# Scaled expert inputs made by GpSimd instead of VectorE, and begun earlier from the fourth token pair on

## The chip, the cores and the metric

One core of a Trainium2 chip. The metric is device time in microseconds (us) of one execution of the whole program, lower is better. Engines are named as in the profile: PE (TensorE: matmuls, with PEld for its weight loads), DVE (VectorE), ACT (ScalarE), POOL (GpSimd), SP (SyncE, here only a DMA queue). Each engine works through its own instruction stream in order; semaphores tie the streams together.

## What is computed

Two stages, the second on the output of the first:

```python
# 1. attention: q, k, v of shape (4, 8, 768, 64); causal. Heads 0, 2, 6 see all keys
#    before the query, the others 4 sink keys and a window of 64 keys.
a = softmax(where(mask, q @ k.T / 8, -1e9));  attn = a @ v
# 2. four experts over x = attn as (3072, 512); w1 (4, 512, 1024), w2 (4, 1024, 512)
p = domain_probs / (domain_probs.sum(-1, keepdims=True) + 1e-9)
for e in range(4):
    h = np.maximum(x @ w1[e], 0.0)
    out += p[:, e:e + 1] * (h @ w2[e])
```

Since p is not negative, p * relu(x @ w1) = relu((p * x) @ w1). The kernel uses this: for most tokens it multiplies the input by the expert's p ahead of the first layer, and then adds up all experts in one product of the second layer.

## The kernel before

**Tokens.** 3072 tokens are 24 tiles of 128. The attention runs in eight groups of three tiles (four batches, two halves each). Tiles 0 to 3 go through the experts in a plain way; the other twenty go in ten pairs of two tiles, in the code by their first tile: `pairs = [4, 6, ..., 22]`. The program works on the experts of one pair while it works on the attention of a later group: their matmuls are interleaved on PE in an order that Python code writes out by hand (`manual_schedule`: each engine gets its instructions in the order in which the code emits them). Each `yield` of the generators `moe_steps` and `attention` lets the other go on, by a plan with a due time for each attention group.

**A pair** (`pair_steps`). Layer 1 runs expert by expert: `plain_layer1` for experts 0, 1, 2 and, for expert 3 (and in the last three pairs for more of them), `winograd_layer1`, a Strassen-Winograd form with seven products instead of eight. Layer 2 is one such form over all experts: six `product` calls of 16 matmuls of 256 columns and a seventh one, with sums on DVE in between.

**Scaled inputs** (`scale_inputs`). For a pair and an expert, xs = xT * pB: xT is the attention's output, transposed, in fp16 (one tile per attention group), pB the pair's probabilities for all partitions in fp32. One instruction of 128 x 1024 elements, or two of 512 where the pair lies in two groups (pairs 8, 14, 20). `xs` has three slots: experts 0 and 2 share one, expert 1 has the second, expert 3 the third. So expert 2's input may be written only when PE has read expert 0's. In the last pairs expert 2 goes to a tile of its own, `xs1`, that takes the room of q's tile, and in the last two expert 1 goes into a part of `vS`. `scaled_sums` makes sums of an expert's scaled input on DVE for the Winograd form. `pB` has one buffer: `load_probs` of the next pair on SP waits until this pair's last input is made.

In the kernel before, the inputs of experts 0 and 3 of the next pair are made on DVE after the fifth and the sixth product of layer 2, those of experts 1 and 2 within layer 1 of the pair (in the last pairs somewhat differently).

**POOL** issues the attention's loads as DMAs: when the code takes up a group it calls `loads`, three DMAs for `k_rows` (L219), three for `q` (L219), three for `vR` (L304); after each window head's product of probabilities and values it calls `load_v` for the next group's `vS` (L306, five for a group). A vS load waits until PE has read that head's old values (L828). SP transposes k, q and the attention's output by DMA (`transpose_rows`, L790) and stores the results.

Lines that come up later: L1180 the scaling, L1196, L1204 and L1014 sums and differences on DVE, L1229 and L1258 the matmuls of layer 1 (plain, Winograd), L1409 those of layer 2, L693 the attention's scores, L756 and L828 its values, L718 and L722 its masks.

Of the kernel before, what the change touches and what calls it, by code (L numbers as in the profile page):

```python
# [19 lines left out]
def kernel(  # L20
# [33 lines left out]
    nc = tc.nc  # L54
# [43 lines left out]
    gp = nc.gpsimd  # L98
# [15 lines left out]
    EW = (E - 1, E - 2)  # L114
# [291 lines left out]
    for h in range(H):  # L406
# [16 lines left out]
        eng = nc.scalar if h < HP else nc.sync  # L423
# [131 lines left out]
    def mm_ns(cols):  # L555
        return cols / 2.4 + 2.5
# [444 lines left out]
    S2, S3, S4 = A11, A21, A12  # L1001
# [141 lines left out]
    def pieces(nt0):  # L1143

        g0, j0 = divmod(nt0, 3)
        n0 = min(3 - j0, PT)
        yield g0, j0 * P, 0, n0
        if n0 < PT:
            yield g0 + 1, 0, n0, PT - n0
# [16 lines left out]
        x = xs_of[0][:, n * DMP * PC : (n + 1) * DMP * PC]  # L1166
        return x.rearrange("p (c x) -> p c x", c=DMP)

    def scale_inputs(nt0, e):

        if xs_of[0] is None:
            xs_of[0] = moe.tile([P, XS], FP16, name="xs", tag="xs", bufs=1)
        xs = scaled(e)
        for g, c0, t0, n in pieces(nt0):
            require(g)
            xin = xT[g][:, :, c0 : c0 + n * P].rearrange("p c (t x) -> p c t x", t=n)
            o = xs[:, :, t0 * P : (t0 + n) * P].rearrange("p c (t x) -> p c t x", t=n)
            pb = pB_of[nt0][:, t0 : t0 + n, e, :]
            pb = pb.rearrange("p t (c x) -> p c t x", c=1)
            nc.vector.tensor_tensor(  # L1180
                out=o, in0=xin, in1=pb.to_broadcast([P, DMP, n, P]), op=ALU.mult
            )

# [30 lines left out]

    def two(nt0):
        return nt0 >= pairs[-LAST]

    def three(nt0):
        return nt0 >= pairs[-2]

    def pair_steps(nt0, nxt):
# [93 lines left out]
        a, b = (winograd_layer1(e, *y) for e, y in zip(EW, (banks, banks[::-1])))  # L1315
        if three(nt0):
# [5 lines left out]
            b = winograd_layer1(EW[1], *more_banks, more_kept)  # L1322
# [19 lines left out]
        if not two(nt0):  # L1342
            n = itertools.chain(*(plain_layer1(e) for e in range(E - 1)))
            order = (
                ((n,), lambda: scale_inputs(nt0, 1)),
                ((n,), more[0] if more else None),
                ((n, a), lambda: last_weight_sum(E - 1) if nt0 == pair0 else None),
                ((n, a), None),
                ((n, a), lambda: scale_inputs(nt0, 2)),
                ((n, a), lambda: load_probs(nxt)),  # L1350
                ((n, a), more[1] if more else None),
                ((n, a), more[2] if more else None),
                ((n, a), lambda: first_sum(0, 2)),
                ((n,), None),
                ((n, n), lambda: first_sum(2, 2)),
                ((), lambda: scale_inputs(nxt, 1) if two(nxt) else None),
            )
        elif nxt is None:
            order = (
                ((), lambda: scaled_sums(EW[1])),  # L1360
                ((a, b, a, b), None),
                ((a, b, a, b), lambda: scaled_sums(EW3)),
                ((a, b, a, b, a, b), lambda: scaled_sums(0)),
                ((third, fourth, third, fourth), lambda: first_sum(EW[0])),
                ((third, fourth, third, fourth), lambda: first_sum(EW[1])),
                ((third, fourth, third, fourth), None),
                ((third, fourth), lambda: (first_sum(EW3), first_sum(0))),
            )
        elif three(nt0):
            n = plain_layer1(0)  # L1370
            order = (
                ((), lambda: scaled_sums(EW[1])),
                ((a, b, a, b), lambda: load_probs(nxt)),
                ((a, b, a, b), None),
                ((a, b, a, b), None),
                ((a, b), lambda: scaled_sums(EW3)),
                ((n,), more[0]),
                ((third, third, n), lambda: first_sum(EW[0])),
                ((third, third, n), more[1]),
                ((third, third, n), lambda: (first_sum(EW[1]), first_sum(0))),  # L1380
                ((third,), lambda: (first_sum(EW3), more[2]())),
            )
        else:
            n = itertools.chain(plain_layer1(0), plain_layer1(1))
            order = (
                ((a, a, n), more[0] if more else None),
                ((a, a, n), lambda: load_probs(nxt) if nxt else None),
                ((a, a, n), more[1] if more else None),
                ((n,), lambda: scaled_sums(EW[1])),
                ((a, b, n), more[2] if more else None),  # L1390
                ((b, b, n), lambda: first_sum(0)),
                ((b, b, n), lambda: first_sum(EW[0])),
                ((b, n, b), lambda: (first_sum(1), first_sum(EW[1]))),
            )
# [9 lines left out]
        x = pO.tile([P, DM], FP32, name="pO", bufs=2)[:, 0:HN]  # L1404
        y = pO.tile([P, DM], FP32, name="pO", bufs=2)[:, 0:HN]

        def product(ps, a, b, first, middle=None):
            for k in range(KT):
                nc.tensor.matmul(  # L1409
                    out=ps,  # L1410
                    lhsT=a[:, k, :],
                    rhs=b(k),
                    start=(first and k == 0),
                    stop=(k == KT - 1),
                    skip_group_check=not first,
                )
                if k == KT // 2 - 1:
                    if middle is not None:
                        middle()
                    yield KT // 2 * mm_ns(HN), PSHARE  # L1420

        def b(k, n):
            return lambda kt: whole_b(k, n, kt // HT, kt % HT)
# [17 lines left out]
        def second_sum(n):  # L1441
            k = slice(n * KT // 2, (n + 1) * KT // 2)
            minus(S2[:, k, :], S1[:, k, :], A11[:, k, :])

        def third_sum(n):

            k = slice(n * KT // 2, (n + 1) * KT // 2)
            minus(S3[:, k, :], A22[:, k, :], S2[:, k, :])

        def fourth_sum(n):  # L1450
            k = slice(n * KT // 2, (n + 1) * KT // 2)
            minus(S4[:, k, :], A12[:, k, :], S2[:, k, :])

        last = nxt is None
        ahead = nxt and two(nxt)
        if ahead and three(nxt):
            inputs_for_third()
        half = KT // 2 * mm_ns(HN), PSHARE
        yield from product(x, A11, b(0, 0), True)
        keep(0, x)  # L1460
        second_sum(0)
        yield half
        yield from product(y, A12, b(1, 0), True, lambda: second_sum(1))
        add(0, y, 0, 0)
        if ahead and two(nt0):
            scale_inputs(nxt, 1)
        yield half
        yield from product(x, S2, t(1), False, lambda: third_sum(0))
        keep(1, x)
        third_sum(1)  # L1470
        yield half
        yield from product(y, S1, t(0), True, lambda: fourth_sum(0))
        keep(2, y)
        fourth_sum(1)
        yield half
        yield from product(
            x, S3, b(0, 1), False, lambda: scale_inputs(nxt, EW[0]) if ahead else None
        )
        add(2, x, 1, 1)
        if last:  # L1480
            keep(3, x)
        else:
            scale_inputs(nxt, 0)
        yield half
        yield from product(
            y, S4, b(1, 1), False, lambda: scaled_sums(EW[0]) if ahead else None
        )
        add(1, y, 0, 1)
        if nxt is not None:
            scale_inputs(nxt, EW[1] if ahead else EW[0])  # L1490
        store(0)
        if last:
            store(1, 1)
# [28 lines left out]
    pairs = list(range(pair0, NTILE, PT))  # L1522

    def moe_steps():

        sums = []
        for e in range(E):
            n0 = (e % 2) * FTP * CH
            for n, step in enumerate(plain_steps(0, 3, e, lambda: xT[0], n0)):
                yield step  # L1530
                if e == 0 and n == FTP // 2:
                    prob_rows()
                if sums and n >= FTP and n % 2 == 0:
                    sums.pop(0)()
            sums = weight_sums(e)
        for x in sums:
            x()
        sums = first_weight_sums(EW[0])
        for e in range(E):
            n0 = (e % 2) * FTP * P  # L1540
            for n, step in enumerate(plain_steps(3, 1, e, lambda: xT[1][:, :, 0:P], n0)):
                yield step
                if n == FTP - 1:
                    sums[e]()
            if e + 1 < E:
                last_weight_sum(e)
                (
                    lambda: scale_inputs(pairs[0], 0),
                    lambda: scale_inputs(pairs[0], EW[0]),
                    lambda: scaled_sums(EW[0]),  # L1550
                )[e]()
        for n, nt0 in enumerate(pairs):
            yield from pair_steps(nt0, pairs[n + 1] if n + 1 < len(pairs) else None)
# [114 lines left out]
```

## Time and profile before

| what | value |
|---|---|
| time, median of 3 runs | 376.0 us (375.86 to 377.12) |
| span of the profiled execution | 376.1 us |
| granted TensorE clock, mean | 1.000 |
| PE busy | 367.1 us, 98% |
| DVE busy | 281.6 us, 75% |
| ACT busy | 227.3 us, 60% |
| POOL busy (with the issue of its DMAs) | 112.9 us, 30% |
| L1180 on DVE | 49 instructions into xs, 47.0 us; 3 into vS, 2.5 us |
| POOL's loads of vS (L306) | 30, of 0.99 us each; 110.5 us of waits for PE in front of them |

The profile is of one execution and its span agrees with the runs. Its page has the busy time of each engine, the chain of work that ended last and the costliest groups of instructions; further answers of the trace are the timeline of a stretch (start, duration, engine, line, operation, output<-inputs, and in brackets the idle time before it and what ended it), the busy time by stretches of the run, and the waits of one engine (who waited for whom: us in total, times, longest).

### The profile page before, as it was taken

How to read it: one execution, taken by the hardware profiler on the slowest of the kernel's cores; microseconds unless marked ns; L12 is line 12 of the kernel's file. 1: busy time of each engine (PE TensorE's matmuls, PEld its weight loads, DVE VectorE, ACT ScalarE, POOL GpSimd, SP SyncE). 2: the span in 40 equal slices, each digit the busy share in tenths (PEclk: the TensorE clock that was granted, in tenths of full speed). 3: DMA queues.
4: the chain of work that ended last, by engine and by line, in shares of the span. 5: the costliest groups of instructions: out<-in, count | busy, mean ns of one | idle time of the engine just before them, and what ended most of it. 6: DMA issues, size and time to landing. Idle time of an engine off the chain costs nothing.

```text
span 376.1 us, 10310 instructions
## 1 busy us (share of the span) xinstructions
PE 367.1 (98%) x4221; PEld 312.4 (83%) x4221; DVE 281.6 (75%) x589; ACT 227.3 (60%) x475; POOL 112.9 (30%) x155
## 2 busy tenths in 40 slices
PE   8889999999999999999999999999999999999996
PEld 4755556568998999999989899988899998998996
DVE  7774768697788569868657858957767968989882
ACT  3863478557785785765676955774678362450630
POOL 8923664793058038115601650320000000000000
DMA  8999999999599579988904991971220200300101
GB/s 157 159 208 207 179 186 194 180 201 121 90 104 164 97 83 133 153 111 63 205 12 61 169 156 16 131 129 12 68 72 2 92 24 2 114 2 0 58 3 58
DMA packets 123748, 39.25 MB, mean 104 GB/s; under 512 B 113728, under 2 KB 116356, under 8 KB 123700
## 3 DMA queue, kind: packets, MB, share of 16 engines
q0 software_dynamic: 85824, 19.01, 58.6%
q1 hardware_dynamic: 36276, 19.18, 23.3%
q8 instruction: 33, 0.54, 0.7%
q10 hardware_dynamic: 1600, 0.39, 0.5%
q14 instruction: 15, 0.12, 0.1%
HBM read 44.89 MB, written 6.34 MB: 136 GB/s over the span
## 4 chain that ended last, share of the span: by engine, by line
PE 78%; DMA 12%; DVE 5%; POOL 3%; issue 1%; ACT 0%; DVEq 0%; POOLq 0%
PE pO L1409 29%; PE pA L1229 20%; PE pO L1258 9%; PE pO L1116 5%; DMA q<-in_q_dram 5%; PE pA L693 4%; DMA w2sb<-in_moe_w_dram 4%; PE pA L1095 3%; DMA w1sb<-in_moe_w_dram 2%; PE pV L1258 2%; PE pA L1258 2%; DVE xs L1180 2%; PE pV L828 2%; PE pV L756 2%; DMA xT<-x_pair 1%
## 5 line engine op out<-in xcount | busy, mean ns | idle before, releaser
L1409 PEld LDWEIGHTS <-hA 128*128 128x128 f16 x1104 | 104.9, 98 | 11.9
L1229 PE MATMUL pA<-xs,w1sb 128*128 128x256 f16 x768 | 97.1, 272 | 0.0
L1229 PEld LDWEIGHTS <-w1sb 128*128 128x128 f16 x768 | 71.7, 98 | 7.3
L1409 PE MATMUL pO<-w2sb,hA 128*128 128x256 f16 x640 | 76.8, 272 | 0.0
L711 ACT ACTIVATE es<-pA 128x384 f16<-128x384 f32 (+2 forms) x122 | 59.2, 512 | 26.4 <-PE pA L693 23.2
L1238 ACT ACTIVATE hA<-pA 128x512 f16<-128x512 f32 x96 | 57.2, 597 | 29.6 <-PE pA L1229 27.3
L306 POOL DMA_DIRECT2D vS<-in_v_dram x30 | 29.6, 986 | 113.7 <-PE pV L828 110.5
L1409 PE MATMUL pO<-tsb,hA 128*128 128x256 f16 x464 | 56.8, 272 | 0.0
L1180 DVE TENSOR_TENSOR xs<-xT,pB 128x1024 f16<-128x1024 f16 (+1 forms) x49 | 47.0, 977 | 3.7 <-DMA xT<-x_pair 3.7
L1014 DVE TENSOR_TENSOR hA<-hA 128x1024 f16<-128x1024 f16 x60 | 39.4, 684 | 0.6 <-PE pO L1409 0.3
L1108 ACT ACTIVATE hA<-pA 128x384 f16<-128x384 f32 (+1 forms) x64 | 22.2, 385 | 20.3 <-PE pA L1095 20.2
L1258 PEld LDWEIGHTS <-w1sb 128*128 128x128 f16 x512 | 31.3, 98 | 2.1 <-DVE xs L1014 0.8
L1095 PE MATMUL pA<-xT,w1sb 128*128 128x384 f16 (+1 forms) x256 | 30.4, 272 | 2.0 <-DMA w1sb<-in_moe_w_dram 1.9
L1116 PE MATMUL pO<-w2sb,hA 128*128 128x512 f16 x128 | 30.6, 379 | 0.1
L1095 PEld LDWEIGHTS <-w1sb 128*128 128x128 f16 x256 | 19.5, 98 | 11.0 <-issue 2.6
L1429 ACT COPY s<-pO 128x256 f32<-128x256 f32 x31 | 11.5, 372 | 27.3 <-PE pO L1409 21.8
L851 DVE TENSOR_TENSOR xT<-pV,rc 64x384 f16<-64x384 f32 x37 | 20.5, 554 | 9.3 <-ACT rc L856 6.8
L722 DVE TENSOR_TENSOR es<-es,mS 128x384 f16<-128x384 f16 (+1 forms) x40 | 13.8, 344 | 18.0 <-ACT es L711 17.9
L846 ACT ACTIVATE rc<-pV,eps 64x384 f32<-64x384 f32 x37 | 21.3, 575 | 7.0 <-PE pV L828 6.4
L1275 DVE CUSTOM_DVE_ANT_0 hA<-pO,s 128x512 f16<-128x512 f32 x26 | 17.7, 688 | 9.9 <-PE pO L1258 8.5
L1268 ACT COPY s<-pO 128x512 f32<-128x512 f32 x39 | 22.7, 588 | 3.2 <-PE pO L1258 3.0
L693 PE MATMUL pA<-qT,kR 128*128 128x128 f16 (+2 forms) x141 | 23.1, 261 | 0.4 <-DVE kR L602 0.4
(170 smaller groups left out, 527.6 us busy)
## 6 DMA issues: line engine op xcount, KB each, us to landing
pB<-p_rows SPq DMA_DIRECT2D x10, 512.0 KB
out_dram<-o SPq DMA_DIRECT2D x19, 256.0 KB
w1sb<-in_moe_w_dram POOLq DMA_DIRECT2D x8, 512.0 KB, 9.2
w2sb<-in_moe_w_dram POOLq DMA_DIRECT2D x4, 1024.0 KB, 13.3
vS<-in_v_dram POOLq DMA_DIRECT2D x30, 112.0 KB, 4.8
k_rows<-in_k_dram POOLq DMA_DIRECT2D x18, 128.0 KB, 5.1
q<-in_q_dram POOLq DMA_DIRECT2D x18, 128.0 KB, 6.4
vR<-in_v_dram POOLq DMA_DIRECT2D x24, 48.0 KB, 5.5
```

The lines of the kernel that those rows point to most:

```text
L306: gp.dma_start(out=t[:, :, own_v(h)], in_=windows_of(v, b, h, c))
L693: nc.tensor.matmul(out=ps[:, o : o + nq], lhsT=key_tile(b, c, h, t), rhs=qTs[b, c][:, hp, q0 : q0 + nq], start=(n == 0 or not first), stop ...
L711: nc.scalar.activation(out=es[:, 0:cols], in_=ps[:, 0:cols], func=AF.Exp, scale=SC)
L1014: nc.vector.tensor_tensor(out=out, in0=a, in1=b, op=ALU.subtract)
L1095: nc.tensor.matmul(out=pss[ft][:, 0:cols_n], lhsT=w1_tile(e, ct, ft), rhs=x[:, ct, :], start=(n == 0), stop=(n == DMP - 1),)
L1116: nc.tensor.matmul(out=ps_o, lhsT=hs[:, ft, j * P : (j + 1) * P], rhs=w2sb[:, e * FTP + ft, :], start=(ft == 0), stop=(ft == FTP - 1),)
L1180: nc.vector.tensor_tensor(out=o, in0=xin, in1=pb.to_broadcast([P, DMP, n, P]), op=ALU.mult)
L1229: nc.tensor.matmul(out=ps[:, f * PC : (f + 1) * PC], lhsT=w1_tile(e, ct, f0 + f), rhs=xs[:, ct, :], start=(ct == 0), stop=(ct == DMP - 1),)
L1238: nc.scalar.activation(out=blocks[:, b0 : b0 + 2, k0 : k0 + 2, :].rearrange("p t f x -> p f t x"), in_=ps.rearrange("p (f t x) -> p f t x" ...
L1258: nc.tensor.matmul(out=ps[:, f * P : (f + 1) * P], lhsT=w_tile(e, w[:, ct, :], f), rhs=a[:, ct, :], start=(first and f == 0 and ct == 0), ...
L1268: nc.scalar.copy(out=kept[n], in_=ps)
L1409: nc.tensor.matmul(out=ps, lhsT=a[:, k, :], rhs=b(k), start=(first and k == 0), stop=(k == KT - 1), skip_group_check=not first,)
```

## The change

The scaling goes from DVE to POOL, save for the two inputs of the first pair (experts 0 and 3) that are made during the plain tiles. And the places where the code emits it are another: the list `to_scale` holds what is to be made for the next pair during layer 2 of this one. For the pairs 6 and 8 these are experts 3 and 0, in the middle of and after the fifth product. For pairs from 10 on (`ahead_of`), they are emitted after the first, third and fourth product, and expert 1's is among them; for the last pairs also expert 2's, in the middle of the fifth product or after it.

```diff
-    def scale_inputs(nt0, e):
+    def scale_inputs(nt0, e, eng=None):
...
-            nc.vector.tensor_tensor(
+            (eng or gp).tensor_tensor(
                 out=o, in0=xin, in1=pb.to_broadcast([P, DMP, n, P]), op=ALU.mult
             )
...
+    def ahead_of(nt0):
+
+        return nt0 >= pairs[3]
...
-                ((n,), lambda: scale_inputs(nt0, 1)),
+                ((n,), lambda: None if ahead_of(nt0) else scale_inputs(nt0, 1)),
...
+        to_scale = []
+        if nxt is not None:
+            to_scale = [EW[0], 0]
+            if ahead:
+                to_scale += [EW[1], 1] if two(nt0) else [EW[1]]
+            elif ahead_of(nxt):
+                to_scale += [1]
+
+        def scale_one(after):
+            if to_scale and (after or ahead_of(nxt)):
+                scale_inputs(nxt, to_scale.pop(0))
+
         yield from product(x, A11, b(0, 0), True)
         keep(0, x)
         second_sum(0)
+        scale_one(False)
         yield half
         yield from product(y, A12, b(1, 0), True, lambda: second_sum(1))
         add(0, y, 0, 0)
-        if ahead and two(nt0):
-            scale_inputs(nxt, 1)
         yield half
         yield from product(x, S2, t(1), False, lambda: third_sum(0))
         keep(1, x)
         third_sum(1)
+        scale_one(False)
         yield half
         yield from product(y, S1, t(0), True, lambda: fourth_sum(0))
         keep(2, y)
         fourth_sum(1)
+        scale_one(False)
         yield half
-        yield from product(
-            x, S3, b(0, 1), False, lambda: scale_inputs(nxt, EW[0]) if ahead else None
-        )
+        yield from product(x, S3, b(0, 1), False, lambda: scale_one(True))
         add(2, x, 1, 1)
         if last:
             keep(3, x)
         else:
-            scale_inputs(nxt, 0)
+            scale_one(True)
...
         add(1, y, 0, 1)
-        if nxt is not None:
-            scale_inputs(nxt, EW[1] if ahead else EW[0])
...
-                    lambda: scale_inputs(pairs[0], 0),
-                    lambda: scale_inputs(pairs[0], EW[0]),
+                    lambda: scale_inputs(pairs[0], 0, nc.vector),
+                    lambda: scale_inputs(pairs[0], EW[0], nc.vector),
```

In the built program the streams of PE, ACT and SP hold the same instructions in the same order as before. 50 instructions of L1180 have left DVE's stream; the rest of it is unchanged. On POOL's stream they stand between the DMAs, in this order for the pairs by their first tile (numbers are experts; "loads" are the nine DMAs of k_rows, q and vR of the next group, "vS" one load of L306):

```
pair 4:   loads, 1, 2
pair 6:   vS x5, 3, loads, 0, 1, 2
pair 8:   vS x5, loads, 3, 0, 1, 2      (each in two halves)
pair 10:  3, vS, 0, vS, 1, vS x3, loads, 2
pair 12:  3, 0, 1, vS x4, 2, vS, loads
pair 14:  3, 0, 1, vS x2, 2, vS x2      (each in two halves)
pair 16:  3, vS, 0, 1, 2
later:    no loads between them
```

## The prediction

> **What bounds the kernel now.** I read first the page's busy times and the share of each stretch, then the waits of PE, then the chain, then the queue orders around the moved instructions, and last the timeline at each place where a moved result is read.
>
> ```profile
> PE 367.1 (98%) x4221; PEld 312.4 (83%) x4221; DVE 281.6 (75%) x589; ACT 227.3 (60%) x475; POOL 112.9 (30%) x155
> ...
> 80.00:110.00 30.00, 30.00 (x373) 25.75 (x372) 24.08 (x51) 20.78 (x50) 10.31 (x13) 1.00 1.09 129
> ...
> 230.00:260.00 30.00, 29.52 (x362) 26.74 (x360) 23.57 (x56) 19.23 (x38) 4.94 (x5) 1.00 0.66 89
> ...
> PE pO L1258 <- DVE xs L1014: 0.5, 1, 0.5
> PE pO L1258 <- ACT hA L1308: 0.2, 1, 0.2
> ```
>
> PE is the bound, and really so: in the pairs it is busy for whole stretches (second number of a stretch), and the chain steps at one rate (48 matmuls of 256 columns in 5.24 us at 253.47, 112 in 12.23 us at 310.55: 109 ns each). From 80 us on PE waits 0.5 us for DVE once and 0.2 us for ACT once; those two lines are the whole list. So relieving DVE can win 0.7 us at most, 0.2% of 376. Less than 0.3% (1.1 us) can't be told from no change here. What can move the time is a new wait of PE.
>
> **What the change moves.** 50 of the 52 instructions of L1180 (47.0 us for 49 by the page's group, 2.5 us for the three into vS) leave DVE for POOL; the first pair's inputs of experts 0 and 3 stay. The order of PE, ACT and SP is as before. DVE loses 26 whole pieces of 1.21 us and 24 half pieces of 0.68 us, 48 us that stand beside PE: worth 0, bound 0.7. The cost is where they go: POOL also issues the attention loads, in order, and holds each until PE has freed its buffer.
>
> **The price of one on POOL.** No row shows a product of two inputs there. From below: DVE's own 1.21 us. From above: GpSimd's select, one input, took 654 ns for 504 elements (1.30 ns each); if two inputs are read one after the other, 1024 elements take 2.66 us. I take the middle between one stream (1.33) and two (2.66), 2.0 us, as GpSimd need not slow a select and a product alike; half pieces by DVE's ratio 0.68/1.21, 1.12 us. The Trainium skill (GPSIMD Engine Reference, § 3.1 Elementwise) has a 2048-element product-like add at 4497 ns, 1.96 times VectorE; an estimate from it is 2.2 us, and the time below would be 0.9 us more.
>
> ```profile
> L1180 DVE TENSOR_TENSOR xs<-xT,pB 128x1024 f16<-128x1024 f16 (+1 forms) x49 | 47.0, 977 | 3.7 <-DMA xT<-x_pair 3.7
> ...
> L491 POOL TENSOR_SCALAR_AFFINE_SELECT mS<-mS 128x504 f16<-128x504 f16 x1 | 1.0, 985 | 0.1
> L487 POOL TENSOR_SCALAR_AFFINE_SELECT mS<-mS 128x504 f16<-128x504 f16 x1 | 0.7, 654 | 0.1
> ```
>
> **Second pair (tiles 6, 7).** On POOL's new queue stand: five vS loads, expert 3's input, nine loads (k_rows, q, vR: three each), then the inputs of experts 0, 1, 2. PE's first matmul of the pair reads expert 0's.
>
> ```profile
> 112.08 0.98 POOL L306 DMA_DIRECT2D vS<-in_v_dram  x1 [0.46 <-issue]
> ...
> 113.06 2.65 POOL L219 DMA_DIRECT2D k_rows<-in_k_dram  x3
> ...
> 115.33 1.23 DVE L1180 TENSOR_TENSOR xs<-xT,pB 128x1024 f16<-128x1024 f16 x1 [0.55 <-DMA xT<-x_pair]
> ...
> 115.67 2.66 POOL L219 DMA_DIRECT2D q<-in_q_dram  x3
> ...
> 118.27 2.39 POOL L304 DMA_DIRECT2D vR<-in_v_dram  x3
> ...
> 118.81 1.91 PE L1229 MATMUL pA<-xs,w1sb 128*128 128x256 f16 x16
> ```
>
> The bracket at 115.33 is the point: DVE stood idle there until the last transpose of xT landed, so no engine can scale this pair earlier. Now POOL waits to 115.33 with expert 3's input (done at 117.3, before DVE's sums want it at 118.21), and the nine loads behind it, which began at 113.06 and took 7.60 us in a row (to 120.66), follow. Expert 0's input is done at 115.33 + 2.0 + 7.60 + 2.0 = 126.9; PE wants it at 118.81. New wait: 8.1 us. Expert 1 then follows 2.0 later, 3.2 before PE reaches it (5.2 after its first, 124.05); expert 2 likewise fits. The loads land some 4 us later and PE is 8.1 later, so nobody waits for them.
>
> **Third pair (8, 9).** Here all nine loads stand ahead of all its inputs, each in halves (its tiles are of two attention groups).
>
> ```profile
> 144.35 2.65 POOL L219 DMA_DIRECT2D k_rows<-in_k_dram  x3
> ...
> 146.84 1.28 DVE L1180 TENSOR_TENSOR xs<-xT,pB 128x512 f16<-128x512 f16 x2
> 146.96 2.66 POOL L219 DMA_DIRECT2D q<-in_q_dram  x3
> ...
> 149.55 1.91 PE L1229 MATMUL pA<-xs,w1sb 128*128 128x256 f16 x16
> 149.55 2.33 POOL L304 DMA_DIRECT2D vR<-in_v_dram  x3
> ```
>
> The loads follow a vS load that PE frees, so they keep their place relative to PE. They end at 151.88; two halves of expert 3 and two of expert 0 take 4 x 1.12: 156.4, wanted at 149.55. New wait: 6.8 us. DVE's sums of expert 3 and the masks queued behind them wait less than PE does.
>
> **From the fourth pair on.** The products in front give cover; I checked each reader. Fourth: experts 3, 0, 1 stand among vS loads and are done near 173 for a reader at 178.16; expert 2 behind the loads (end 184.53) at 186.5 for 188.27. That cover is 1.7 us: gone if a piece costs over 3.7. Fifth: 198 for 209.70; its expert 2 must wait for PE to leave the slot (213.98) and holds one vS and nine loads by 3 us, landing near 231 for transposes at 233. Sixth: 231 for 238.51; its expert 2 goes into q's old room, free only where DVE began at 247.18 before, done by 249.4 for a reader at 249.19: 0 to 0.2, against the 0.5 us wait for DVE that goes: 0. It holds two vS loads to 249, whose buffer is read only after the sink rows of 269. Seventh to tenth: five or more us early. First pair: 89.8 for 93.44 and 94.8 for 99.38. SP's pB load of the next pair waits for POOL's last input of this one (expert 2), in the fourth pair 1.8 us longer than for DVE's; what stands behind it on SP is an xT transpose of 197.31, twelve us on, and the pB itself is wanted by the early products only, so nothing is late.
>
> **After a stall.** PE has no row of a pause over 1.3 us in its work. Its nearest long rest is the one ahead of its first matmul, and there it ran at half rate:
>
> ```profile
> 1.27 3.59 PE L448 MATMUL pO<-early 128*128 128x512 f16 x8 [1.27 <-DVE early L433]
> ...
> 69.90 4.32 PE pO L1116 x20
> ```
>
> Eight matmuls of 512 columns from 1.27 to 4.73, 0.43 us each, against 0.216 later; full rate from about 6.5. That costs half of 5.2 us, 2.6. After the 1.1 us wait at 21.5 the rate was full. Bounds for each stall: 0 to 2.6; stalls of 8 and 7 us resemble the rest more than the 1.1 us wait, so I take 2.6 twice, 5.2. The Trainium skill (TensorE: Matmul & The Clock Gate, Part 1) says the same of the sign: an idle window of about 3.4 us halves the clock until about 3.4 us of sustained work; by that figure it would be 1.7 twice, 1.8 us less in all. The trace's start agrees (half rate, for 5.2 us); no run here shows it within the work.
>
> **Sum.** Profiled execution 376.1 us, median of the runs 376.0, so nothing lies around the span; from the median: 376.0 + 8.1 + 6.8 + 5.2 = 396.1, said as 396.
>
> **Rivals.**
> *Stalls without the half rate*: 376.0 + 14.9 = 390.9. For it: the 1.1 us wait cost nothing afterwards. Against: the start.
> *DVE and POOL hold each other up.* DVE's two sums at 75.64 took 2.17 us beside L491 of POOL, where L1014 has 0.684 each: 0.8 lost. If in each of the seven later pairs one sum on PE's path loses that, 5.6 more: 401.7. Against: DVE is given 48 us. The Trainium skill (SBUF — State Buffer, Who interferes with whom) states it as a rule: a VectorE instruction with two SBUF inputs and a GpSimd instruction that reads SBUF exclude one another; the row agrees.
> *Not slower: loads do not hold the scaling.* If POOL only hands a load over and computes beside its 0.8 to 1 us, the nine loads cost nothing: second pair 115.33 + 4.0 = 119.3 for 118.81, third 145.7 (xT written) + 4.5 = 150.2 for 149.55; 1.2 us, less up to 0.7: 376.5. It decides below 1.74 us a piece, where the second wait is gone too. Against: POOL's rows of loads, and of memset and load at 85.5, begin where the last ends.
>
> **Chances.** Forecast 0.62; full rate after 0.25; hindrance 0.08; loads beside scaling 0.05. The range runs from the second case at 1.2 us a piece (6.5 + 5.0, 387.5) to the forecast at 2.66 (9.4 + 8.3 + 5.2, 399) with some hindrance: 387 to 401. The last rival is split between same (0.03) and faster (0.02, where all 0.7 and more comes back); slower 0.95.
>
> **What would show it.** PE's waits get two lines for the layer-1 matmul on POOL's xs, near 8.1 and 6.8; POOL has 50 products of about 2.0 and 1.12 us with nine loads between experts 3 and 0 of the second pair; 256-column matmuls right after the stalls step by 213 ns for some 5 us, elsewhere by 109. No such waits, or like ones from the fourth pair on, would make me wrong.

## The result and the profile after

The changed kernel takes 426.2 us (median of four runs, 425.2 to 426.7) against 376.6 us for the kernel before (375.9 to 377.6): 1.132 times as long, 95% interval 1.129 to 1.134. The prediction was 396.0 us with a range of 387 to 401. The sign was right, the size was not: of about 50 us more, 20 were forecast. The profiled execution has a span of 424.9 us, 48.8 more than before.

First the page after: the engines' busy line (with share of the span and count of instructions), and the TensorE clock in forty slices.

```profile
PE 380.9 (90%) x4221; PEld 318.3 (75%) x4221; DVE 291.8 (69%) x539; ACT 227.4 (54%) x475; POOL 199.7 (47%) x205
...
PEclk9999999999978995998999996998999999998999
```

DVE has given 50 instructions to POOL (589 to 539), and yet its busy time has grown from 281.6 to 291.8 us. That is the first sign that a busy row is not work done: what was left on DVE has become slower. PE is busy for 90% where it was 98%, and its clock, 1.000 on average before, has dips.

The list of PE's waits (total us, times, longest) shows two families. Before, it had nothing of this size.

```profile
PE pO L1413 <- DVE hA L1014: 19.8, 6, 5.0
PE pA L1233 <- POOL xs L1180: 13.0, 2, 6.8
PE pV L828 <- DVE xT L851: 2.0, 1, 2.0
```

The second line is the forecast pair of stalls. The first and larger one was not in the sum: the second layer waits for sums that DVE makes. (Lines from L1217 on are four higher than before; in some experiments added lines shift them a little further.) The groups, with shapes kept apart, give both prices: count, busy us, mean ns of one, then idle time ahead.

```profile
L1180 POOL TENSOR_TENSOR xs<-xT,pB 128x1024 f16<-128x1024 f16 x25 | 56.1, 2258 | 67.6 <-PE pA L1233 29.4 <-PE pO L1262 23.8 <-PE pV L756 4.8
L1014 DVE TENSOR_TENSOR hA<-hA 128x1024 f16<-128x1024 f16 x60 | 50.8, 875 | 0.3
L1204 DVE TENSOR_TENSOR hA<-hA 128x1024 f16<-128x1024 f16 x14 | 26.6, 1897 | 4.4 <-ACT hA L1242 4.4
```

A scaling costs 2.26 us on POOL, 2.13 at best. A sum of L1014 cost 0.684 us before and costs 0.875 on average now. The same row of the kernel before:

```profile
L1014 DVE TENSOR_TENSOR hA<-hA 128x1024 f16<-128x1024 f16 x60 | 39.4, 684 | 0.6 <-PE pO L1409 0.3
```

The 14 whole sums of L1204 average 1.90 us, where an undisturbed one in the same trace takes 0.68.

The timeline at the second pair (start, duration, engine) shows the forecast queue as it was drawn: one scaling, nine loads, then expert 0's scaling, for which PE waits.

```profile
113.14 2.26 POOL L1180 TENSOR_TENSOR xs<-xT,pB 128x1024 f16<-128x1024 f16 x1 [0.84 <-DVE xT L851]
115.35 3.05 POOL L219 DMA_DIRECT2D k_rows<-in_k_dram  x3
118.39 2.63 POOL L219 DMA_DIRECT2D q<-in_q_dram  x3
120.98 2.28 POOL L304 DMA_DIRECT2D vR<-in_v_dram  x3
123.27 4.24 POOL L1180 TENSOR_TENSOR xs<-xT,pB 128x1024 f16<-128x1024 f16 x2
125.47 3.57 PE L1233 MATMUL pA<-xs,w1sb 128*128 128x256 f16 x16 [6.29 <-POOL xs L1180]
```

The last line also shows half rate: 16 matmuls in 3.57 us, where 16 took 1.91 before.

The timeline in the fourth pair shows what was not foreseen.

```profile
184.63 1.04 POOL L306 DMA_DIRECT2D vS<-in_v_dram  x1 [2.11 <-PE pV L828]
185.01 6.51 DVE L1014 TENSOR_TENSOR hA<-hA 128x1024 f16<-128x1024 f16 x1
185.69 2.15 POOL L1180 TENSOR_TENSOR xs<-xT,pB 128x1024 f16<-128x1024 f16 x1
187.78 1.02 POOL L306 DMA_DIRECT2D vS<-in_v_dram  x1
188.83 2.14 POOL L1180 TENSOR_TENSOR xs<-xT,pB 128x1024 f16<-128x1024 f16 x1
191.59 1.68 PE L1413 MATMUL pO<-tsb,hA 128*128 128x256 f16 x7 [4.27 <-DVE hA L1014]
```

A sum of 0.68 us begins at 185.01 and ends at 191.52, half a microsecond after POOL's second scaling. PE, which reads it, stands for 4.3 us. The same happens at 249.47 (a sum of 6.68 us, beside six half-size scalings) and at 287.00 (6.48 us, beside three whole ones).

Copies, which read one operand, are held too. Beside the first scaling of the second pair two copies of keys take 2.46 us together, the second of them 2.18 where it took 0.24 before:

```profile
113.06 2.46 DVE L274 COPY kR<-kT 64x768 f16<-64x768 f16 x2
```

PE waits behind them, at 116.02 us.

At last come the windows behind four ends of waits. The columns are the window, its length, PE's busy time and matmuls, four other engines, and PEclk, third from the end.

```profile
125.40:129.00 3.60, 3.53 (x19) 2.47 (x19) 0.00 (x0) 0.60 (x1) 2.11 (x2) 0.50 0.19 15
191.50:195.00 3.50, 3.42 (x21) 2.49 (x22) 3.36 (x8) 0.00 (x0) 0.00 (x0) 0.53 0.03 5
328.90:332.40 3.50, 3.50 (x43) 3.18 (x43) 3.37 (x7) 2.42 (x5) 0.00 (x0) 1.00 0.00 0
386.40:389.90 3.50, 3.42 (x19) 2.50 (x20) 3.36 (x7) 0.09 (x1) 0.00 (x0) 0.58 0.00 0
```

Behind a wait of 6.3, 4.3 and 4.3 us the clock is about a half; behind the wait of 2.0 us (328.9) it is whole.

PE runs the same 4221 matmuls in the same order in both kernels, so the difference of their starts is the account of the loss. Each wait is a step in it; half rate is the slope behind a step.

| Part of the 48.8 us | us |
|---|---|
| Two waits for POOL's scalings: 6.5, 6.9 | 13.4 |
| Half rate behind them: 2.1, 2.7 | 4.8 |
| Four long waits for held sums, at 191, 258, 294, 386 us: 4.4, 5.1, 5.2, 4.4 | 19.1 |
| Half rate behind them: 1.6, 2.5, 1.5, 1.4 | 7.0 |
| Six short waits behind DVE's work beside POOL's or the backlog that it left (the first in the second pair, behind the copies): 1.0, 0.5, 0.4, 2.2, 0.9, 1.1 | 6.1 |
| Small steps, gains for the most part, half of them ahead of 60 us | -1.6 |

The first two rows were forecast at 20.1 us and came to 18.2. The next three, 32.2 us, were not in the forecast.

### The profile page after: what moved, and what is told of

It reads as the page before. It is cut to its first block, busy times and chain, and to the rows that moved or that the text cites. A ratio compares the mean times of both kernels' runs of the same rounds, so it can differ in the third digit from the quotient of the medians.

```text
span 424.9 us, 10344 instructions
## 1 busy us (share of the span) xinstructions
PE 380.9 (90%) x4221; PEld 318.3 (75%) x4221; DVE 291.8 (69%) x539; ACT 227.4 (54%) x475; POOL 199.7 (47%) x205
## 4 chain that ended last, share of the span: by engine, by line
PE 61%; issue 11%; POOL 9%; DVE 8%; DMA 8%; ACT 2%; SPq 0%; POOLq 0%; DVEq 0%; ACTq 0%
PE pO L1413 18%; PE pA L1233 17%; PE pO L1262 7%; DMA w2sb<-in_moe_w_dram 6%; PE pO L1116 5%; PE pA L1095 4%; DVE hA L1014 3%; PE pA L693 3%; PE pV L1262 2%; POOL vR L304 2%; DVE hA L1204 2%; POOL xs L1180 2%; PE pA L1262 1%; DMA xT<-x_pair 1%; POOL k_rows L219 1%
## 5 line engine op out<-in xcount | busy, mean ns | idle before, releaser
L1413 PEld LDWEIGHTS <-hA 128*128 128x128 f16 x1104 | 107.7, 101 | 37.0 <-DVE hA L1014 21.3
L1180 POOL TENSOR_TENSOR xs<-xT,pB 128x1024 f16<-128x1024 f16 (+1 forms) x47 | 82.0, 1770 | 95.5 <-PE pA L1233 34.4
L1233 PE MATMUL pA<-xs,w1sb 128*128 128x256 f16 x768 | 101.7, 281 | 13.0 <-POOL xs L1180 13.0
L1233 PEld LDWEIGHTS <-w1sb 128*128 128x128 f16 x768 | 73.6, 100 | 22.8 <-issue 13.4
L1413 PE MATMUL pO<-tsb,hA 128*128 128x256 f16 x464 | 63.4, 292 | 20.6 <-DVE hA L1014 19.8
L711 ACT ACTIVATE es<-pA 128x384 f16<-128x384 f32 (+2 forms) x122 | 59.3, 512 | 34.8 <-PE pA L693 31.5
L306 POOL DMA_DIRECT2D vS<-in_v_dram x30 | 29.9, 997 | 60.2 <-PE pV L828 58.2
L1014 DVE TENSOR_TENSOR hA<-hA 128x1024 f16<-128x1024 f16 x60 | 50.8, 875 | 0.3
L1204 DVE TENSOR_TENSOR hA<-hA 128x1024 f16<-128x1024 f16 (+1 forms) x26 | 36.8, 1422 | 5.2 <-ACT hA L1242 5.1
L1262 PEld LDWEIGHTS <-w1sb 128*128 128x128 f16 x512 | 31.3, 98 | 2.1 <-DVE xs L1014 0.9
L851 DVE TENSOR_TENSOR xT<-pV,rc 64x384 f16<-64x384 f32 x37 | 20.5, 554 | 15.9 <-ACT rc L856 13.5
L722 DVE TENSOR_TENSOR es<-es,mS 128x384 f16<-128x384 f16 (+1 forms) x40 | 15.4, 388 | 19.9 <-ACT es L711 19.8
L1095 PEld LDWEIGHTS <-w1sb 128*128 128x128 f16 x256 | 19.5, 98 | 10.3 <-issue 1.9
```

Source lines behind the costliest of these rows:

```text
L306: gp.dma_start(out=t[:, :, own_v(h)], in_=windows_of(v, b, h, c))
L711: nc.scalar.activation(out=es[:, 0:cols], in_=ps[:, 0:cols], func=AF.Exp, scale=SC)
L1014: nc.vector.tensor_tensor(out=out, in0=a, in1=b, op=ALU.subtract)
L1095: nc.tensor.matmul(out=pss[ft][:, 0:cols_n], lhsT=w1_tile(e, ct, ft), rhs=x[:, ct, :], start=(n == 0), stop=(n == DMP - 1),)
L1180: (eng or gp).tensor_tensor(out=o, in0=xin, in1=pb.to_broadcast([P, DMP, n, P]), op=ALU.mult)
L1204: nc.vector.tensor_tensor(out=S1[:, k, :], in0=A21[:, k, :], in1=A22[:, k, :], op=ALU.add)
```

## The experiments

The theory after this reading: GpSimd's scalings hold VectorE's instructions that read two operands from SBUF. The rivals were the new places of the scalings, and GpSimd's slowness alone. The whole change was first taken apart.

**The places alone** (edit against the changed kernel):

```diff
-            (eng or gp).tensor_tensor(
+            nc.vector.tensor_tensor(
```

> All scalings at the changed kernel's places, but on VectorE. Holding theory (a GpSimd product holds VectorE's instructions with two SBUF inputs, PE then waits for the sums; and the product itself is late behind nine loads in the pairs of tiles 6 and 8): no GpSimd product, so no new wait, 376 us within 2. Place theory (the earlier places are what hurts: the scalings are queued ahead of the sums of layer 2 on whatever engine makes them): seven pairs in which 1.2 to 3.6 us of scalings stand in front of the sums that PE wants next; 390 to 405 us, with PE waits for L1014.

Measured: 382.5 us, 1.016 times before (1.013 to 1.019). That is between the two expectations and fits neither well: the places cost some 6 us of their own while DVE does the scaling. The timeline shows how.

```profile
174.61 1.21 DVE L1180 TENSOR_TENSOR xs<-xT,pB 128x1024 f16<-128x1024 f16 x1
175.85 0.56 DVE L851 TENSOR_TENSOR xT<-pV,rc 64x384 f16<-64x384 f32 x1
176.47 0.34 PE L828 MATMUL pV<-es,vS 128*128 128x48 f16 x7 [0.56 <-DVE xT L851]
```

A scaling of 1.21 us now stands in DVE's queue ahead of an attention step that PE needs next. Eleven delays of PE of 0.3 to 0.9 us add up to 6.6 us.

**The engine alone**, in the places of before (edit against the kernel before; the first pair's two early inputs stay on VectorE):

```diff
-            nc.vector.tensor_tensor(
+            (eng or gp).tensor_tensor(
...
```

> The places of the kernel before, but GpSimd makes all scalings save the first pair's two. Holding theory: the products now stand between layers, where fewer sums are on PE's path, but late for their readers: expert 0's comes 4 to 5 us late behind the loads in the pairs of tiles 6 and 8, about 1 to 2 us late in the others; with half rate after the two long stalls and some held sums 395 to 415 us, PE waiting for xs of GpSimd more than for L1014. Place theory: the engine does not matter but for lateness, 376 + about 20 us.

Measured: 424.5 us, 1.126 (1.123 to 1.130): above the range expected, and nearly the whole loss. Here three scalings are late by 15.3 us in all, and two sums by 13.0. So the engine makes the loss in either order; the new places only trade one kind of wait for the other.

**GpSimd from the fourth pair on**, VectorE for the first three, all in the new places, and **its mirror image**:

```diff
-            (eng or gp).tensor_tensor(
+            (gp if ahead_of(nt0) else nc.vector).tensor_tensor(
```

```diff
-            (eng or gp).tensor_tensor(
+            (eng or (nc.vector if ahead_of(nt0) else gp)).tensor_tensor(
```

> The changed kernel, with GpSimd making only the scalings of the pairs from tile 10 on. Holding theory: PE's two waits for xs of GpSimd (13.0 us) and the half rate after them (4.8) are gone, the waits for the sums stay (about 25 us, and 8 of half rate): 408 us within 4. If instead the later waits were a consequence of the first two stalls (loads and transposes thrown out of step), they go too: 376 to 382.

> The changed kernel, with GpSimd making the scalings of the pairs of tiles 4, 6 and 8 only. Holding theory: only the two waits for xs of GpSimd stay, 6.5 and 6.9 us, and half rate after each, 2.1 and 2.7: 376.5 + 18 = 394.5 us within 2; this is what the prediction had summed up. If the two stalls were themselves lengthened by what the later pairs do, less: 385 to 390.

Measured: 409.2 us, 1.086 (1.083 to 1.089), and 399.6 us, 1.064 (1.057 to 1.071). The first is as expected. The second is 5 us more than expected, about what the places alone cost in the experiment above; PE's short waits for DVE are nearly those of that experiment (1.5 us for L1436 here, 1.8 there; 1.3 for L851 in both). Measured from the places alone, GpSimd's part in the first three pairs is 399.6 - 382.5 = 17.1 us and in the later ones 409.2 - 382.5 = 26.7 us; together 43.8, and the whole change is 43.7 above it. The two halves add up. PE's waits in the first of them (sums, no scalings) and in the mirror image (scalings, no long wait for sums):

```profile
PE pO L1413 <- DVE hA L1014: 19.8, 6, 5.0
PE pV L828 <- DVE xT L851: 2.0, 1, 2.0
```

```profile
PE pA L1233 <- POOL xs L1180: 13.1, 2, 6.8
```

**GpSimd that only writes** (against the kernel with GpSimd from the fourth pair on; the scaling of the later pairs is left out here and in the next experiment):

```diff
-            (gp if ahead_of(nt0) else nc.vector).tensor_tensor(
+            if ahead_of(nt0):
+                for _ in range(2):
+                    gp.memset(o, 0.0)
+                continue
+            nc.vector.tensor_tensor(
```

> As the kernel with GpSimd from the pair of tile 10 on only, but in place of each product GpSimd writes zeros to the same output twice (about 2 us, nothing read): the scaling of those pairs is left out. Holding theory with the shared reading side: VectorE's sums are not held, L1014 and L1204 at 0.68 us, no PE wait for L1014: 376 to 379 us. If it is GpSimd's writing, or its presence on the semaphores and in the queue, that holds VectorE: about 400 to 410 as with the products.

Measured: 377.7 us, 1.004 (1.001 to 1.007), as expected. The largest wait for DVE behind the first microseconds is now

```profile
PE pO L1417 <- DVE o L1440: 1.1, 2, 0.8
```

The same places and about the same time on POOL's queue, but no reading, cost next to nothing. This also says that the places cost 6 us only where DVE does the scaling. Against this kernel, the products of the later pairs cost 409.2 - 377.7 = 31.5 us; the account above has 31.2 for them (32.2 less the 1.0 in the second pair). Copies did feel the writing: one of L274 that took 0.24 us before took 1.08 beside the memsets, off PE's path.

**GpSimd that reads one operand:**

```diff
...
+                for _ in range(2):
+                    gp.tensor_copy(out=o, in_=xin)
...
```

> As the kernel with GpSimd from the pair of tile 10 on only, but in place of each product GpSimd copies the input xT to the same output twice (one SBUF input, no probability: the scaling of those pairs is left out). Holding theory, any reading by GpSimd holds VectorE: PE waits for L1014 like those with the products where the copies last as long (if a copy takes 1.1 us, two of them hold as long as one product: 400 to 410 us). If only an instruction with two inputs on GpSimd holds VectorE: 376 to 380.

Measured: 391.7 us, 1.040 (1.036 to 1.045), between the two. One operand read is enough to hold DVE: the waits for L1014's sums are 4.6 us in seven, and none is over 2.0 us. Reading holds VectorE's sums, writing does not.

**The pause filled** (against the kernel with GpSimd in the first three pairs only): 48 matmuls of 256 columns with no use are put in front of the second and the third pair's first matmul, so that PE works through its wait.

```diff
+        if nt0 in pairs[1:3] and e == 0 and f0 == 0:
+            for _ in range(48):
+                nc.tensor.matmul(
+                    out=ps[:, 0:PC], lhsT=w1_tile(0, 0, 0),
+                    rhs=w1sb[:, 0, 0:PC], start=True, stop=True)
```

> As the kernel with GpSimd for the pairs of tiles 4, 6 and 8 only, with 48 matmuls of 256 columns more (5.2 us of PE, results overwritten) in each of the two waits ahead of the first matmul of the pairs of tiles 6 and 8. If PE falls to half rate after a pause, the added matmuls keep it at full rate and the time is some 4 to 5 us shorter than without them, about 390 us; if the slow stretches come from something else, the same time, about 394.5.

Measured: 397.7 us, 1.056 (1.042 to 1.070, two runs): by time alone not told apart from 1.064. The profiles tell more. Both windows begin at the end of the second pair's wait, the unfilled kernel first:

```profile
125.30:128.80 3.50, 3.44 (x17) 2.45 (x17) 0.00 (x0) 0.60 (x1) 2.11 (x2) 0.50 0.25 19
```

```profile
125.00:128.50 3.50, 3.03 (x33) 2.71 (x33) 0.00 (x0) 1.20 (x3) 2.51 (x2) 1.00 0.49 31
```

33 matmuls run at full clock instead of 17 at half. The spans of these two executions differ by 397.7 - 393.9 = 3.8 us, but the second execution of the filled kernel was 4.2 us longer than the profiled one, so the times alone show nothing. The starts of PE's own matmuls, compared as above, do: the filled kernel gains 1.7 us at the second pair and 2.5 at the third, and under 0.1 behind that, of the 4.8 that half rate cost in the changed kernel.

**A measurement of the hold and of the pause**, in a program of its own (one execution, as with the two measuring programs that follow).

> Not the kernel but its parts alone: none of the attention or the experts is computed. Nine stages: VectorE sums of 1024 fp16 elements alone; GpSimd products alone; both at once; VectorE with one input in PSUM beside GpSimd products; VectorE sums beside GpSimd memsets; beside GpSimd copies; beside products with a load issued between them; beside quarter products; and TensorE bursts of 80 matmuls with pauses of 1 to 7 us. Holding theory: sums 0.68 us alone, products about 2.15 us alone; together a sum that meets a run of products lasts until the run ends or nearly (over 4 us); one input in PSUM and memsets beside: as alone; copies: held. Theory of a lock by the instruction: a sum waits for one product at most (2.2 us) and the two engines alternate. TensorE: half rate for the matmuls after a pause from some length between 1.5 and 4 us on, full rate after shorter ones.

VectorE's sums (two operands of 128x1024 from SBUF) take 0.68 us each, GpSimd's products 2.13 us each, alone. Together, started at the same time (12 sums, 4 products); then DVE's instructions with one operand in PSUM beside products; then sums beside GpSimd's memsets:

```profile
26.91 9.74 POOL L73 TENSOR_TENSOR po<-x,pb 128x1024 f16<-128x1024 f16 x4 [0.30 <-ACT x L60]
26.96 15.06 DVE L64 TENSOR_TENSOR dout<-d,d 128x1024 f16<-128x1024 f16 x12 [9.11 <-ACT d L61]
...
44.98 6.70 DVE L67 TENSOR_TENSOR fout<-ps,f 128x256 f32<-128x256 f32 x20
...
51.60 7.31 DVE L64 TENSOR_TENSOR dout<-d,d 128x1024 f16<-128x1024 f16 x12
51.65 7.20 POOL L106 MEMSET pm<- 128x1024 f16 x8
```

The first four sums took 2.62 us each, ending 0.5 us behind a product each; the products behind the first took 2.58 instead of 2.13. They took strict turns: one sum, one product. With an operand from PSUM nothing is held (20 in 6.70 us), nor beside memsets (12 in 7.31). Beside copies a sum took 1.52 us, beside quarter products 1.16. Only where loads' issues stood between the products was one sum held for 6.97 us, as in the kernel.

The last stage runs bursts of 80 matmuls with growing pauses (in brackets, PE's idle time ahead of the burst):

```profile
149.49 8.91 PE L136 MATMUL pz<-w 128*128 128x256 f16 x80 [2.64 <-DVE w L143]
161.76 10.57 PE L136 MATMUL pz<-w 128*128 128x256 f16 x80 [3.37 <-DVE w L143]
176.43 11.76 PE L136 MATMUL pz<-w 128*128 128x256 f16 x80 [4.09 <-DVE w L143]
```

Up to 2.64 us of pause a burst takes 8.91 us; from 3.37 us on it takes 10.57, 11.76, 10.33 (4.82 us) and 10.56 (6.28 us). So a pause costs 1.4 to 2.9 us more from some point between 2.64 and 3.37 us on, and the length of it does not matter beyond that. The Trainium skill (TensorE: Matmul & The Clock Gate, Part 1) puts the point at about 3.4 us of idle time. The runs here agree within their steps: it lies above 2.64 and not above 3.37 us.

**Where does a sum lose more than one turn?** Single sums at chosen times, without loads between the products:

> A measurement, not the reference's work: single VectorE sums (128x1024, two SBUF inputs, 0.68 us alone) set at chosen times against three GpSimd products in a row, then eight sums beside six issues of loads without products, then a sum begun during a load's issue in front of product, load, product. In the kernel after, some sums were held for one product (2.6 us) and others for the whole run of products (6.5 us); the records do not say why. Theory 'order': a sum that is under way when a product begins loses its turn to every product of the run (5 to 7 us), and one that begins while a product runs gets its turn when that product ends (between 0.7 and 2.7 us, less the later it begins). Rival 'chance of the meeting': the place of the sum does not decide, so that sums on both sides of the product's start are held now for one product, now for three. Rival 'last tenths': only a sum that begins so that it would end just as a product ends or begins loses all turns. For the loads alone: sums stay at 0.6 to 0.7 us each, if a load's issue by itself holds nothing; 1.5 us or more, if it holds them.

```profile
43.01 0.69 DVE L64 TENSOR_TENSOR dout<-d,d 128x1024 f16<-128x1024 f16 x1 [6.52 <-ACT d L61]
...
43.49 6.38 POOL L73 TENSOR_TENSOR po<-x,pb 128x1024 f16<-128x1024 f16 x3
...
50.17 6.76 POOL L73 TENSOR_TENSOR po<-x,pb 128x1024 f16<-128x1024 f16 x3 [0.30 <-ACT x L60]
50.22 2.63 DVE L64 TENSOR_TENSOR dout<-d,d 128x1024 f16<-128x1024 f16 x1 [6.52 <-ACT d L61]
```

A sum begun first was not held (0.69 us); the first product took 2.20 to 2.52 us instead. One begun behind the product's start ended 0.5 us behind that product wherever it was put: 2.63 us down to 0.84. No sum was held for two products. Of theory "order" the second half stands, and the first half falls with both rivals. Sums beside six loads' issues without products kept 0.69 us. The last trial, a sum begun during an issue in front of a product, missed: the sum was over (134.09) as the issue began (134.08). So what was missing here was a load in front of products.

**A load's issue in front of the products:**

> A measurement, not the reference's work. In after, e3 and m1 the long holds (6.5 to 7.0 us of one VectorE sum) all stand where GpSimd's product follows directly on a load's issue and VectorE was in the middle of an instruction; in m2 sixteen single sums, none of them across a load's issue, were held for one product at most. Each trial here has one sum (0.68 us alone): A, begun during a load's issue, with one, two, three, four or six whole products behind it; B, the same with eight half and sixteen quarter products; C, a memset of 0.95 us in the place of the issue; D and E, the sum begun a little behind the product's start, with VectorE busy or idle across it; F, a memset between the issue and the products; G, two issues. Theory 'issue': the issue of a load directly in front is the condition. Then A is held for 2.5, 4.6 and 6.5 us with one, two and three products and not longer than about 7 us with four and six, if the like lengths of the four long holds mean a limit of time; C and F show 0.7 to 2.7 us. Rival 'run': a sum under way is held to the end of the run, so A with six products is held for some 13 us. Rival 'no issue needed': C is held as long as A with four products.

```profile
42.50 13.47 DVE L64 TENSOR_TENSOR dout<-d,d 128x1024 f16<-128x1024 f16 x1
42.84 12.58 POOL L73 TENSOR_TENSOR po<-x,pb 128x1024 f16<-128x1024 f16 x6
...
68.00 0.72 DVE L64 TENSOR_TENSOR dout<-d,d 128x1024 f16<-128x1024 f16 x1
68.34 10.36 POOL L73 TENSOR_TENSOR po<-x,pb 128x256 f16<-128x256 f16 x16
...
79.72 0.68 DVE L64 TENSOR_TENSOR dout<-d,d 128x1024 f16<-128x1024 f16 x1
80.01 8.65 POOL L73 TENSOR_TENSOR po<-x,pb 128x1024 f16<-128x1024 f16 x4
```

With a load's issue in front, a sum of 0.68 us is held to the end of the whole run of products: 5.1, 7.2, 9.3 and 13.5 us with two, three, four and six, and 9.9 us with eight half products (the trial with one product says nothing on this: the product began 3.5 us behind the issue, the sum 1.0 us behind the product's start, and it took 1.7 us). The hold is the same whether the sum begins during the issue or up to 0.9 us behind the product's start. With a memset in the place of the issue it is not held (third couple of lines), nor with quarter products (second couple). So in these trials a load's issue in front is needed for the long hold, and there is no limit of time; on that the rival "run" was right. It is not the whole condition. In the kernel with the engine alone a sum begun in the middle of a load's issue, directly in front of four half-size products, took 1.18 us, and the two engines went on by turns:

```profile
245.90 1.18 DVE L1204 TENSOR_TENSOR hA<-hA 128x1024 f16<-128x1024 f16 x1 [3.28 <-ACT hA L1238]
246.39 6.08 POOL L1180 TENSOR_TENSOR xs<-xT,pB 128x512 f16<-128x512 f16 x4
```

One part of the theory fell: with a memset between issue and products the sum was still held, for 9.1 us. Why the issue takes away VectorE's turns, what else that needs, and why quarter products give them back, no run here shows.

**Quarter products in the kernel** (against GpSimd from the fourth pair on):

```diff
...
+                for c in range(DMP):
+                    gp.tensor_tensor(
+                        out=o[:, c : c + 1], in0=xin[:, c : c + 1],
+                        in1=pb[:, c : c + 1], op=ALU.mult,
+                    )
...
```

> As e3 (pairs one to three scaled on VectorE, the others on GpSimd with the new places), but every GpSimd product cut into four pieces, one for each 128 rows of the input, issued back to back. In the measurement alone a sum beside such pieces took 1.16 us against 2.62 us beside whole products. If VectorE takes turns with GpSimd at the end of every piece, TensorE's waits for sums (19.8 us in e3) shrink to some 4 to 8 us and the time is 380 to 393 us. If a sum in the kernel is held for the whole run of GpSimd's products however they are cut, as the one was that stood through five half-size products in a row, the waits stay and the time is 405 to 413 us.

Measured: 381.4 us, 1.013 (1.011 to 1.015), as the first theory expected, against 409.2 with whole products. PE's waits:

```profile
PE pO L1419 <- DVE o L1442: 1.7, 3, 0.8
...
PE pO L1419 <- DVE hA L1014: 0.7, 1, 0.7
```

19.8 us of waits for L1014's sums have become 0.7, with the same engine, the same places and the same work. This is the clearest proof that the hold, not GpSimd's speed, made the loss of the later pairs. VectorE still loses time: its 86 sums into hA (L1014 and L1204) take 70.6 us, against 55.7 before and 89.6 with whole products. But none is longer than 1.17 us, where the longest was 6.69, and PE hardly waits. The kernel is still 3.7 us above the one that only writes; its list has short waits of at most 1.1 us, and what the rest is stays open.

**A memset in front of each product** (against the same kernel):

```diff
+            if ahead_of(nt0):
+                gp.memset(o[:, 0:1], 0.0)
             (gp if ahead_of(nt0) else nc.vector).tensor_tensor(
```

> As e3, but GpSimd writes zeros to the first quarter of each output (about 0.3 us) directly before each product, so that no product follows directly on a load's issue or on another product. If the long holds need the issue directly in front, or no gap between the products, the three waits of 4.4 to 5.2 us at TensorE and the half rate behind them go (14.7 us and about 6.8 us), and the time is 385 to 392 us against 409 us of e3; the holds of one product each stay. If a sum is held for the whole run whatever stands between, the time is 405 to 413 us.

Measured: 400.1 us, 1.062 (1.058 to 1.066): 9 us less than without, but 8 us above the range expected.

```profile
PE pO L1415 <- DVE hA L1014: 6.2, 5, 4.3
PE pO L1415 <- DVE o L1438: 3.6, 3, 2.4
```

The three waits at the held sums of 6.5 us went, as expected, and no sum is held longer than 2.63 us. The holds of one product each stayed and became more, and the last long wait (4.3 us, now at 359 us, with no load near it) is made of three such holds in a row. The expectation had left them at their old sum. In the measurement above a memset between the issue and the first product did not end the long hold; here there is one between the products too, which may be what gives VectorE its turn. That was not tested by itself.

No version was faster than the kernel before: with PE at 98% there was at most 0.7 us to win.

## Why the prediction was wrong

**What bounds the kernel: right.** PE was the bound, DVE's relief was worth nothing, and all that moved the time was new waits of PE.

**The price of one on POOL: 2.0 us, measured 2.26 on average,** within the bounds of 1.21 to 2.66 (half pieces 1.22, 1.12 forecast). The estimate from the Trainium skill (GPSIMD Engine Reference, § 3.1 Elementwise), 2.2 us, was nearer.

**Second and third pair: right.** 6.5 and 6.9 us for 8.1 and 6.8, in the queue order that was drawn. The first is shorter because POOL began its first scaling at 113.14, not 115.33, directly behind DVE's last write into xT (112.46 + 0.56): the bracket at 115.33 of before had been read as the earliest time for any engine, and was not. PE, 0.8 us earlier by then, also came 1.0 later to its matmul, behind the held copies. Dearer scalings and loads gave 0.7 back; that much of the nearness of 8.1 is luck.

**Half rate: right, but for two stalls of six.** 2.1 and 2.7 us for 2.6 twice. The estimate from the Trainium skill (TensorE: Matmul & The Clock Gate, Part 1) was 1.7 twice, further off. The mechanism held at four more pauses, another 7.0 us, that the sum did not have.

**From the fourth pair on: the step that failed.** "The products in front give cover; I checked each reader" was true of the readers of xs: PE waits for POOL's scalings in the second and third pair alone. But the cover is full of DVE's own sums, which PE also reads, and moving the scalings under that cover put two engines side by side that hold each other up. The mechanism was among the rivals, and it was mis-sized: 0.8 us for one sum in each of seven pairs, 5.6 us, at a chance of 0.08. Measured: 25.2 us of waits (19.1 and 6.1, of which 1.0 in the second pair) and 7.0 of half rate, 32.2 us. The 0.8 came from a row of sums beside selects that read one operand and take 0.65 and 0.98 us. A product takes 2.13 us, and the hold lasts as long as the other's instruction: 2.62 - 0.68 = 1.9 us a turn, up to 6.0 us over a run behind a load's issue. "DVE is given 48 us" is no argument against it, since DVE's queue is in order and PE waits for a certain sum.

**The rule of the Trainium skill** (SBUF — State Buffer, Who interferes with whom) spoke against the change and was given a chance too small. It says that a VectorE instruction with two SBUF operands and a GpSimd instruction that reads SBUF exclude one another for the whole instruction, and that writing alone does not. The runs agree: 2.62 us beside products, 0.68 beside memsets, nothing lost with an operand in PSUM. It also says that who starts first has the pair of ports; the sums begun first and held for 5 to 13 us behind a load's issue do not fit that.

**The last rival,** loads that do not hold the scaling, was wrong: the nine loads took 7.9 us in a row and the scaling came behind them.

## What to carry to other kernels

Before moving work from VectorE to GpSimd, list what VectorE has left to do at that time with two operands in SBUF, and its copies within SBUF, and price each at GpSimd's whole instruction, not at its own; if the tensor engine waits for one of these, the move costs more than the relieved engine can give back. If the move must be made, cut GpSimd's instructions small (a quarter of the size took the waits from 19.8 to 0.7 us here), or keep one of VectorE's operands in PSUM. And count each new pause at the tensor engine of 3.4 us or more at 1.4 to 2.9 us more than its length.

## What the runs showed of the hardware

- In the measuring program a VectorE sum of 0.68 us, begun during a load's issue on GpSimd's queue or up to 0.9 us behind it, with a run of GpSimd products behind the issue, was held to the end of the run, 13.5 us with six products. Without the issue the two engines took turns (2.62 us a sum). Load issues alone held nothing (0.69 us). In the kernel with the engine alone one sum begun in such a place took only 1.18 us.
- With products of a quarter of the size (0.66 us) the long hold did not occur, behind a load's issue either (0.72 us); with eight half-size ones it did (9.9 us).
- A VectorE copy within SBUF, which reads one operand, took 2.18 us beside a product and 1.08 beside memsets, where it takes 0.24.
- Half rate behind a pause begins between 2.64 and 3.37 us of pause, and what it costs (1.4 to 2.9 us) does not grow with the pause.
